# Sparse attention and a feed-forward block on one core: the tiles of two heads alternate, and both heads' products with v run as plain float32 on the two column halves of TensorE

## The chip, the core and the metric

The kernel runs on one core of a Trainium2 chip. The core has a matrix engine (TensorE, PE in the profile, with its weight loads as PEld), three engines for everything else (VectorE or DVE, ScalarE or ACT, GpSimd or POOL), a queue engine for DMAs (SyncE or SP), an on-chip memory (SBUF) of 128 partitions and a smaller one (PSUM) of eight banks, into which alone TensorE writes. The metric is the device time of one execution in microseconds. Engines run their own instruction lists in order and wait for each other by semaphores.

## What is computed

```python
def _attn_ref(q, k, v, tau):              # 8 batches, 8 heads, 576 positions, head size 64
    scores = np.matmul(q, k.transpose(0, 1, 3, 2)) / np.sqrt(64)
    thresh = np.max(scores, axis=-1, keepdims=True) - tau
    scores = np.where(scores >= thresh, scores, -1000000000.0)
    scores = scores - np.max(scores, axis=-1, keepdims=True)
    attn = np.exp(scores)
    attn = attn / (np.sum(attn, axis=-1, keepdims=True) + 1e-09)
    return np.matmul(attn, v)

def _moe_ref(x, w_in, w_out):             # 4608 tokens, 512 -> 2048 -> 512
    h = x @ w_in
    sp = np.where(h > 20.0, h, np.log1p(np.exp(np.minimum(h, 20.0))))
    return (h * np.tanh(sp)) @ w_out
```

The output of attention, heads side by side, is the input x of the second function. All is float32.

## The kernel before

**Stages.** Attention goes over 32 pairs of heads (four pairs a batch); the first large product (h, x times w_in) of one batch runs between the attention tiles of the next batch. When attention is over, the last batch's h follows, then the second large product (o). Only attention and the h among it are touched here.

**A pair and its tiles.** A pair has 2 x 576 = 1152 query rows, cut into nine tiles of 128 rows. `QCOL` says which columns of which head's q a tile takes: tiles 0 to 3 are head 0, tile 4 is the last 64 rows of head 0 and the first 64 of head 1, tiles 5 to 8 are head 1. Tiles are numbered through all pairs by g (0 to 287), and t = g % 9.

**A tile's way.** `begin` issues the scores s on PE (two PSUM tiles, so that s of g + 2 waits for the mask of g). DVE takes the row maximum (`st<-s`), ACT the exponential e, DVE masks and sums (p), POOL normalises. Two steps later PE transposes the tile in four pieces of 128 positions (`tp`, one PSUM tile) and the last 64 positions (t5, named t in the profile). A step later ACT copies the result to SBUF. The normalised tile of an even g stands in the left half of a buffer, that of an odd g in the right half; the scores of even g are computed with the last 64 positions in front (`first` is D), so that two tails lie side by side and one transposition serves two tiles.

**Two kinds of arithmetic.** Pairs 0 to 3 (`FULL`) multiply in plain float32. All others split each operand into a high part (float32r, one fast pass) and a remainder: ACT makes `hi`, DVE makes `lo` (lines 456 to 469), both for the four main pieces and for the tails (`tk`), and POOL and ACT split v into `vs` (128 columns: high and remainder).

**The products with v.** They come in four groups a pair, each of one head: 256, 320, 320 and 256 query rows (`WIDTH`), after tiles 1, 4, 6 and 8 (`LAST`). In pairs from 4 on a group is nine products (`values`): hi and lo for each of four chunks, tk for the last, all with 128 stationary columns. ACT copies the upper and the lower half out of PSUM (`x`, `yo`), POOL adds them. In pairs 0 to 3 a group is five plain products with 64 stationary columns (`values_full`), spread over steps by `PIECES`.

**The order.** One step of the loop (lines 668 to 768) is one g. On PE it issues s of g + 1, the group of products that has come due, so many h products as `MIX` says for this step (twelve h products fill one bank, which ACT then copies to `hst`), and the transpositions of g - 2 (during the first 38 steps these stand ahead of the products). The groups y and the h take turns at two PSUM banks (`psh`, tag `ph`). On ACT a step is: the copies of the transposed tile g - 3, the exponential of g, copies out of y, splits of loaded data, copies of h. `LOADS` gives the step in which each part of the next pair but one is loaded.

Of the kernel before, what the change touches and what calls it, by code (L numbers as in the profile page):

```python
# [17 lines left out]
LOADS = ((1, 0, 1, 3, 2, 3, 7, 3, 5, 8), (0, 3, 3, 2, 5, 4, 5, 8, 5, 7), (0, 0, 2, 4, 5, 4, 7, 6, 7, 8))  # L18
# [4 lines left out]
FIRST = (0, 4, 5, 1, 2, 6, 7, 3, 8, 9)  # L23
# [42 lines left out]
MIX_FIRST = (11, 12, 6, 9, 8, 13, 6, 14, 22, 6, 16, 4, 12, 4, 15, 9, 16, 13, 7, 12, 5, 10, 8, 13, 12, 14, 16, 6, 16, 4, 12, 4, 15, 5, 16, 13)  # L66
# [90 lines left out]
def attention_moe(tc, q, k, v, tau, w_in, w_out, out):  # L157
# [3 lines left out]
    with ExitStack() as outer:  # L161
# [105 lines left out]
        with ExitStack() as first:  # L267
# [6 lines left out]
            with ExitStack() as att:  # L274
# [36 lines left out]
                def prep(pi):  # L311
# [9 lines left out]
                    if full:  # L321
                        made["vf"] = ops.tile([P, 2, 5, D], F32, name="vf", tag="vs")
# [35 lines left out]
                    def v_part(a):  # L358
                        if full:
# [12 lines left out]
                        return split  # L372
# [6 lines left out]
                def scores(t, first, qs, k1, k2, plain, **_):  # L379
                    s = pss.tile([P, 2, 512], F32, name="s")  # L380
                    terms = []
                    if plain:
                        for n, (a, col) in enumerate(QCOL[t]):
                            for c in range(2):
                                rows = slice(c * D, (c + 1) * D)
                                nc.tensor.matmul(
                                    s[:, c, :HB], qs[a][rows, col:col + P], k1[a][rows, first:first + HB],
                                    start=n == 0, stop=n == len(QCOL[t]) - 1,
                                )
                        return s  # L390
                    for a, col in QCOL[t]:
# [37 lines left out]

                def transposes(g):  # L430

                    both = tiles[g]["both"]
                    odd = g % 2
                    at = odd * (S + D)
# [4 lines left out]
                    if g < FULL * 9:  # L439
                        t5 = pst.tile([P, P], F32, name="t5")  # L440
                        nc.tensor.transpose(t5[:D], both[:, 4 * P + odd * D:4 * P + (odd + 1) * D], ident)
                    elif odd:
                        t5 = pst.tile([P, P], F32, name="t5")
                        nc.tensor.transpose(t5, both[:, 4 * P:5 * P], ident)
                    return tp, t5

                def evacuate(t, tp, t5, pt):
                    for r, off, src, n in PLACE[t]:
                        if r not in pt:
                            pt[r] = [ptp.tile([P, w, 320], F32, name="pf", tag=tag) for w, tag in ((4, "hi"), (1, "tk"))]  # L450
                        main, tail = pt[r]
                        dst = slice(off, off + n)
                        nc.scalar.copy(main[:, :, dst], tp[:, :, src:src + n])
                        nc.scalar.copy(tail[:D, 0, dst], t5[:D, src:src + n])
# [33 lines left out]
                def values_full(r, pt, vf, x):  # L488
                    main, tail = pt.pop(r)
                    n = WIDTH[r]  # L490
                    a = r // 2
                    y = psh.tile([P, 512], F32, name="y", tag="ph")

                    def chunk(c):
                        if c < 4:
                            nc.tensor.matmul(y[:D, :n], vf[:, a, c], main[:, c, :n], start=c == 0, stop=False)
                        else:
                            nc.tensor.matmul(y[:D, :n], vf[:D, a, 4], tail[:D, 0, :n], start=False, stop=True)
# [125 lines left out]
                def start_pair(g, pi):  # L624
                    parts, todo = prep(pi)
                    pairs[pi] = dict(ops=parts, pt={})
                    for work, step in zip(todo, LOADS[1 if 2 <= pi < FULL + 2 else pi % 2 * 2]):
                        loads.setdefault(g + step, []).append(work)

                def begin(g):  # L630
                    pi, t = divmod(g, 9)
                    made = pairs[pi]["ops"]
                    tiles[g] = dict(s=scores(t, D if g % 2 == 0 else 0, **made))

                def product(g):
                    pi, t = divmod(g, 9)
                    pr = pairs[pi]
                    if t == 1:
                        pr["x"] = sm.tile([P, S], F32, name="x", bufs=2)
                    if t in LAST:  # L640
                        if pi < FULL:
                            some, gather = values_full(LAST[t], pr["pt"], pr["ops"]["vf"], pr["x"])
                            pieces.extend((work, None) for work in some[:-1])
                            pieces.append((some[-1], (gather, pi if t == 8 else None)))
                        else:
                            adds.append(values(LAST[t], pr["pt"], pr["ops"]["vs"], pr["x"]))

# [20 lines left out]
                for g in range(NT + 5):  # L668
# [4 lines left out]
                    ahead = 2 <= g < FULL * 9 + 2  # L673
                    lag = 4 if g < FULL * 9 + 4 else 5
                    if lag <= g < NT + lag and g != FULL * 9 + 4:
                        product(g - lag)
                    if 3 <= g < NT + 3:
                        old = ((g - 3) % 9, *tiles[g - 3]["tp"], pairs[(g - 3) // 9]["pt"])
                        full = g - 3 < FULL * 9
# [9 lines left out]
                    for _ in range(5 if g >= FULL * 9 + 3 else PIECES[g % 9]):  # L689
# [35 lines left out]
                    if g >= 12 + 9 * FULL and g % 9 == XSPLIT[0]:  # L725
# [17 lines left out]
                    if g < NT:  # L743
# [4 lines left out]
                        if g % 2 == 0:  # L748
                            both = sm.tile([P, 2 * S], F32, name="p", bufs=2)
                        tiles[g]["both"] = both  # L750
                        half = both[:, :S] if g % 2 == 0 else both[:, S:]
# [202 lines left out]
```

## Time and profile before

| | us |
|---|---|
| median of three runs (1333.97 to 1335.15) | 1335.02 |
| profiled execution | 1334.37 |
| its span | 1332.5 |
| tiles 0 to 41, first to last row maximum | 123.0 |
| tiles 42 to 287 | 762.2 |
| a steady batch of 36 tiles | 110.8 |

The profiled execution's span runs from its first to its last instruction; the 1.9 us between it and the execution's time lie around it. A row of the timeline gives start, duration and a group of equal instructions (out<-in, partitions times elements, count). On PE the ends are modelled and overlap the next start, so distances between starts tell what a matmul takes.

### The profile page before, as it was taken

The page shows a single profiled execution, that of the slowest core. Times are in us where ns is not written, and L with a number is a line of the kernel's source. Part 1 is how long each engine was busy: PE and PEld are TensorE (multiplying, and loading weights), DVE is VectorE, ACT ScalarE, POOL GpSimd, SP SyncE. Part 2 cuts the span into 40 slices and gives each one's busy share as a digit, 9 for nine tenths or more (in the row PEclk, how much of TensorE's full clock was granted, in tenths as well). Part 3 has the DMA queues.
Part 4 walks back from the last instruction along what each step waited for, and adds up shares of the span by engine and source line. Part 5 has one row for each costly group of instructions (what it writes and reads, how often), then busy time and mean ns, then how long its engine had stood idle before and what let it go on. Part 6 is the DMA issues. An engine that isn't in the chain of part 4 may idle for free.

```text
span 1332.5 us, 29620 instructions
## 1 busy us (share of the span) xinstructions
PE 1306.9 (98%) x9799; PEld 1232.8 (93%) x9799; DVE 1117.0 (84%) x2964; ACT 983.3 (74%) x2036; POOL 870.3 (65%) x1229
## 2 busy tenths in 40 slices
PE   8997999999999999999999999999999999999998
PEld 6445899999999999999999999999889999999998
DVE  6999999999999999999999999986986666667664
ACT  4888888888888888888888888875655555555552
POOL 3789998778788787887878878753403433543431
PEclk9999999999999999999999999999999999999999
DMA  5323463333333333333333333314744443444440
GB/s 179 103 81 119 113 189 105 107 97 106 103 102 109 96 106 104 101 110 95 106 104 101 113 92 106 99 37 137 244 130 159 134 136 120 134 135 135 143 127 33
DMA packets 151913, 154.90 MB, mean 116 GB/s; under 512 B 35536, under 2 KB 128720, under 8 KB 151760
## 3 DMA queue, kind: packets, MB, share of 16 engines
q1 hardware_dynamic: 151760, 153.00, 38.6%
q8 instruction: 78, 1.28, 0.4%
q14 instruction: 75, 0.61, 0.1%
HBM read 105.78 MB, written 47.19 MB: 115 GB/s over the span
## 4 chain that ended last, share of the span: by engine, by line
PE 90%; DVE 4%; ACT 3%; issue 1%; DMA 1%; POOL 1%; DVEq 0%; POOLq 0%; ACTq 0%
PE h L91 27%; PE o L91 27%; PE s L91 13%; PE y L91 12%; PE tp L91 9%; DVE st L91 1%; PE t L91 1%; ACT e L91 1%; DVE dec L91 1%; DVE p L91 1%; PE warm L91 0%; DVE w2l L91 0%; ACT w L91 0%; POOL s L91 0%; DMA hd<-hst 0%
## 5 line engine op out<-in xcount | busy, mean ns | idle before, releaser
L91 PE MATMUL h<-xh,w1h 128*128 128x288 f32 x1024 | 302.4, 295 | 1.0 <-ACT hst L91 0.9
L91 PE MATMUL h<-xl,w1h 128*128 128x288 f32 x1024 | 302.4, 295 | 0.0
L91 PE MATMUL h<-xh,w1l 128*128 128x288 f32 x1024 | 302.2, 295 | 0.0
L91 POOL TENSOR_SCALAR p<-p,st 128x576 f32<-128x576 f32 x288 | 242.4, 842 | 56.4 <-DVE st L91 30.7
L91 POOL TENSOR_TENSOR z<-z 128x256 f32<-128x256 f32 x128 | 126.1, 989 | 221.3 <-DVE z L91 212.5
L91 DVE SCALAR_TENSOR_TENSOR p<-s,st,e 128x576 f32<-128x576 f32 x288 | 235.1, 816 | 20.7 <-ACT e L91 10.7
L91 PE MATMUL s<-k,q 128*128 128x288 f32 (+1 forms) x1280 | 240.8, 332 | 9.0 <-DVE p L91 8.0
L91 ACT ACTIVATE e<-s,st 128x576 f32<-128x576 f32 x288 | 214.5, 745 | 32.2 <-DVE st L91 25.4
L91 DVE TENSOR_TENSOR gl<-z,gh 128x1792 fp32r<-128x1792 f32 (+1 forms) x72 | 141.3, 1963 | 107.7 <-ACT gh L91 107.7
L91 ACT CAST gh<-z 128x1792 fp32r<-128x1792 f32 (+1 forms) x72 | 116.5, 1620 | 150.2 <-issue 78.5
L91 DVE TENSOR_REDUCE st<-s 128x1 f32<-128x576 f32 x288 | 216.7, 752 | 2.1 <-PE s L91 2.1
L91 DVE TENSOR_TENSOR lo<-tp,hi 128x512 fp32r<-128x512 f32 (+1 forms) x280 | 174.8, 633 | 48.8 <-ACT hi L91 41.7
L91 PEld LDWEIGHTS s<-k,q 128*128 128x128 f32 (+1 forms) x1280 | 169.7, 189 | 35.3 <-DVE p L91 21.0
L91 PEld LDWEIGHTS h<-xh,w1h 128*128 128x128 f32 x1024 | 192.5, 188 | 1.6 <-ACT hst L91 1.6
L91 PEld LDWEIGHTS h<-xh,w1l 128*128 128x128 f32 x1024 | 192.5, 188 | 0.0
L91 PEld LDWEIGHTS h<-xl,w1h 128*128 128x128 f32 x1024 | 192.4, 188 | 0.0
L91 PE MATMUL tp<-ident,p 128*128 128x128 f32 x1152 | 175.2, 275 | 5.2 <-DVE lo L91 2.2
L91 ACT CAST hi<-tp 128x512 fp32r<-128x512 f32 (+1 forms) x280 | 149.8, 546 | 36.5 <-PE tp L91 33.7
L91 PEld LDWEIGHTS tp<-ident,p 128*128 128x128 f32 x1152 | 138.7, 140 | 19.9 <-issue 8.3
L91 POOL TENSOR_TENSOR x<-x,yo 64x256 f32<-64x256 f32 (+1 forms) x112 | 89.8, 802 | 87.8 <-ACT yo L91 85.5
L91 PE MATMUL o<-gh,sl 128*128 128x256 f32 x512 | 144.5, 282 | 0.0
L91 PE MATMUL o<-gl,sh 128*128 128x256 f32 x512 | 143.8, 281 | 0.0
(76 smaller groups left out, 3234.5 us busy)
## 6 DMA issues: line engine op xcount, KB each, us to landing
z<-hd SPq DMA_DIRECT2D x144, 256.0 KB, 3.1
r<-q SPq DMA_DIRECT2D x112, 160.0 KB, 2.3
r<-k SPq DMA_DIRECT2D x112, 160.0 KB, 2.2
out_t<-c SPq DMA_DIRECT2D x36, 256.0 KB, 2.4
r<-v SPq DMA_DIRECT2D x56, 160.0 KB, 2.3
dec<-w_in SPq DMA_DIRECT2D x32, 256.0 KB, 3.3
hd<-hst SPq DMA_DIRECT2D x16, 512.0 KB, 3.3
w<-w_out SPq DMA_DIRECT2D x16, 512.0 KB, 4.5
```

What stands on the lines that cost most here:

```text
L91: made = method(*args, **kwargs)
```

## The change

- All 32 pairs (`VP`) now keep v in float32 and multiply the normalised, transposed tile with it in plain float32. The splits of the transposed tile (lo and tk on DVE) and of v go. The scores stay as they were: plain in pairs 0 to 3, split in the others.
- Tiles of the two heads alternate (`TURN`): even t are head 0, odd t head 1, each with its own 128 rows; the mixed tile is now t = 8. ACT copies an even tile to `hi` and an odd one to `lo` (here just two buffers, one for each head); tails come in pairs, two extra transpositions serve tile 8.
- There are two groups a pair instead of four (`CLOSE`): 256 columns after t = 3, 320 after t = 8. A group has five chunks, and each chunk two products with 64 stationary columns, head 0 into partitions 0 to 63 and head 1 into 64 to 127 of the same bank. One copy takes all 128 partitions out; `yo` and the sums on POOL go.
- That copy is made one step after the group's last product (the list `ready`).
- The number of h a step is `EVEN`: 14, 14, 14, 0, 13, 14, 14, 0, 13 for g % 9 = 0 to 8, as many in all as `MIX`, with none in the two steps that hold a group.
- `LOADS` and `FIRST` bring the second head's q and k earlier; pairs 0 to 3 do two chunks a step (`PIECES`); p has three buffers.

In the steady part, a group on PE. Names: s scores, y a group's bank, vs or vf the values, hi, lo, tk the transposed tile, h the first large product. Before:

```order
L91 MATMUL y_11300<-hi_11084,vs_10608 128x320 [waits Activation_49]
L91 MATMUL y_11300<-lo_11085,vs_10608 128x320
L91 MATMUL y_11300<-hi_11084,vs_10608 128x320
L91 MATMUL y_11300<-lo_11085,vs_10608 128x320
L91 MATMUL y_11300<-hi_11084,vs_10608 128x320
L91 MATMUL y_11300<-lo_11085,vs_10608 128x320
L91 MATMUL y_11300<-hi_11084,vs_10608 128x320
L91 MATMUL y_11300<-lo_11085,vs_10608 128x320
L91 MATMUL y_11300<-tk_11086,vs_10608 128x320
L91 MATMUL h_11286<-xl_8133,w1h_104 128x288
```

Now, the group of 320 columns (the step has no h, so transpositions follow):

```order
L95 MATMUL y_10934<-hi_10700,vf_9885 64x320 [waits Activation_49]
L95 MATMUL y_10934<-lo_10701,vf_9885 64x320
L95 MATMUL y_10934<-hi_10700,vf_9885 64x320
L95 MATMUL y_10934<-lo_10701,vf_9885 64x320
L95 MATMUL y_10934<-hi_10700,vf_9885 64x320
L95 MATMUL y_10934<-lo_10701,vf_9885 64x320
L95 MATMUL y_10934<-hi_10700,vf_9885 64x320
L95 MATMUL y_10934<-lo_10701,vf_9885 64x320
L95 MATMUL y_10934<-tk_10702,vf_9885 64x320 x2
L95 MATMUL tp_10966<-ident_84,p_10808 128x128 [waits Activation_49,Pool_49]
```

Nine products of one head have become ten of 64 columns, one of each head in turn.

The same place on ACT, where y leaves its bank (x). Before, the copies stand in the group's own step, ahead of the next tile's copy (hi):

```order
L91 ACTIVATE e_11315<-s_11252,st_11314 128x576 [waits DVE_49,Activation_49]
L91 COPY x_11141<-y_11300 64x320 [waits PE_49]
L91 COPY yo_11310<-y_11300 64x320 [waits Pool_49]
L91 CAST q0_11214<-r_11220 128x320 [waits DMAHW3_49]
L91 CAST q0_11214<-r_11222 128x320 [waits DMAHW4_49]
L91 COPY hst_11231<-h_11286 128x288 [waits PE_49]
L91 CAST hi_11362<-tp_11352 128x4x128 [waits PE_49]
```

Now:

```order
L95 COPY lo_10936<-tp_10966 128x4x128 [waits PE_49]
L95 COPY tk_10937<-t5_10971 128x128 [waits PE_49]
L95 ACTIVATE e_10981<-s_10929,st_10980 128x576 [waits DVE_49,Activation_49]
L95 COPY x_10698<-y_10934 128x320
L95 CAST xh_10990<-x_10698 128x288 [waits Activation_49]
L95 COPY hst_10912<-h_10914 128x288 [waits PE_49]
```

The copy out of y has moved behind the copies of the tile that PE transposes right after the group, and behind the next exponential.

And PE's rows from those transpositions to the next user of y's bank, which is h_11003 (its wait is for the copy x_10698):

```order
L95 MATMUL tp_10966<-ident_84,p_10808 128x128 [waits Activation_49,Pool_49]
L95 MATMUL tp_10966<-ident_84,p_10808 128x128 x3
L95 MATMUL t5_10971<-ident_84,p_10808 128x128
L95 MATMUL s_10973<-k11_10306,q1_10305 128x288 [waits DVE_49]
L95 MATMUL s_10973<-k21_10307,q1_10305 128x288
L95 MATMUL s_10973<-k11_10306,q1_10305 128x288
L95 MATMUL s_10973<-k21_10307,q1_10305 128x288
L95 MATMUL h_10914<-xh_10144,w1h_104 128x288
L95 MATMUL h_10914<-xl_10145,w1h_104 128x288
L95 MATMUL h_10914<-xh_10144,w1l_105 128x288
L95 MATMUL h_11003<-xh_8875,w1h_104 128x288 [waits PE_49,Activation_49]
```

Three h end the bank that was begun ahead of the group, and the fourth begins in y's bank. Before, the group above was followed by eleven h, the transpositions and the scores before h took that bank. After the group of 256 columns it is now ten h.

The diff, cut to its core:

```diff
-PIECES = (3, 3, 3, 3, 4, 2, 3, 4, 3)
+PIECES = 2
+VP = 32
+SOON = 9 * FULL + 2
+TURN = [[(t % 2, t // 2 * P + t % 2 * P)] for t in range(8)] + [QCOL[4]]
+CLOSE = {3: 0, 8: 1}
+EVEN = (14, 14, 14, 0, 13, 14, 14, 0, 13)
...
+                    whole = pi < VP
+                    made["cols"] = TURN if whole else QCOL
...
+                def odd(g):
+                    return (g % 9 if g < 9 * VP else g) % 2
...
+                    last = g < 9 * VP and g % 9 == 8
+                    if odd(g) or last:
                         t5 = pst.tile([P, P], F32, name="t5")
+                        if last:
+                            nc.tensor.transpose(t5, both[:, S - P:S], ident)
+                            nc.tensor.transpose(t5[:D], both[:, S - D:S], ident)
+                        else:
+                            nc.tensor.transpose(t5, both[:, 4 * P:5 * P], ident)
...
                 def evacuate(t, tp, t5, pt):
...
+                    if t < 8:
+                        a, at = t % 2, t // 2 % 2 * P
+                        nc.scalar.copy(pt[r][a][:, :, at:at + P], tp)
+                        if a:
+                            nc.scalar.copy(tail[:, at:at + P], t5)
+                        return
+                    for a in range(2):
+                        rows = slice(a * D, (a + 1) * D)
+                        nc.scalar.copy(pt[r][a][:, :, 2 * P:], tp[:, :, rows])
+                        nc.scalar.copy(tail[rows, 2 * P:], t5[rows, rows])
...
                     def chunk(c):
+                        for a in range(2):
+                            rows = slice(a * D, (a + 1) * D)
+                            if c < 4:
+                                w, m = vf[:, a, c], main[a][:, c, :n]
+                            else:
+                                w, m = vf[rows, a, 4], tail[rows, 0, :n]
+                            nc.tensor.matmul(y[rows, :n], w, m, start=c == 0, stop=c == 4)
 
                     def gather():
-                        nc.scalar.copy(x[a * D:a * D + D, XOFF[r]:XOFF[r] + n], y[:D, :n])
+                        nc.scalar.copy(x[:, r * QT:r * QT + n], y[:, :n])
...
-                        advance(stream, DRAIN if g >= NT else MIX_FIRST[(step + 6) % 36] if b == 1 else MIX[g % 18] if b < B - 1 else MIX_LAST[step])
+                        advance(stream, DRAIN if g >= NT else EVEN[g % 9] if b == 1 or VP == NPAIRS else MIX[g % 18] if b < B - 1 else MIX_LAST[step])
```

More of the change, by code (lines that the diff above doesn't have):

```diff
@@ L358, in v_part @@
                     def v_part(a):
-                        if full:
+                        if whole:
                             nc.sync.dma_start(made["vf"][:, a], v[pi, :, a])
@@ L377, in prep, with scores @@
                     return made, loads
-                def scores(t, first, qs, k1, k2, plain, **_):
+                def scores(t, first, qs, k1, k2, plain, cols, **_):
                     s = pss.tile([P, 2, 512], F32, name="s")
@@ L387, in scores @@
                                     s[:, c, :HB], qs[a][rows, col:col + P], k1[a][rows, first:first + HB],
-                                    start=n == 0, stop=n == len(QCOL[t]) - 1,
+                                    start=n == 0, stop=n == len(cols[t]) - 1,
                                 )
                         return s
-                    for a, col in QCOL[t]:
+                    for a, col in cols[t]:
                         cs = slice(col, col + P)
@@ L438, in transposes @@
                     t5 = None
-                    if g < FULL * 9:
+                    last = g < 9 * VP and g % 9 == 8
+                    if odd(g) or last:
                         t5 = pst.tile([P, P], F32, name="t5")
[L441 to L444, printed above, removed]
+                        if last:
[3 more added lines that the diff above has]
+                            nc.tensor.transpose(t5, both[:, 4 * P:5 * P], ident)
                     return tp, t5
                 def evacuate(t, tp, t5, pt):
[L448 to L454, printed above, removed]
+                    r = t // 4 if t < 8 else 1
+                    if r not in pt:
+                        pt[r] = [
+                            ptp.tile([P, w, 320], F32, name=n, tag=n) for n, w in (("hi", 4), ("lo", 4), ("tk", 1))
+                        ]
+                    tail = pt[r][2][:, 0]
+                    if t < 8:
[8 more added lines that the diff above has]
+                        nc.scalar.copy(tail[rows, 2 * P:], t5[rows, rows])
                 def evacuate_hi(t, tp, t5, pt):
@@ L488, in values_full @@
                 def values_full(r, pt, vf, x):
-                    main, tail = pt.pop(r)
-                    n = WIDTH[r]
-                    a = r // 2
+                    main, tail = pt[r][:2], pt.pop(r)[2]
+                    n = (2 + r) * P - r * D
                     y = psh.tile([P, 512], F32, name="y", tag="ph")
                     def chunk(c):
[L495 to L498, printed above, removed]
+                        for a in range(2):
[5 more added lines that the diff above has]
+                            nc.tensor.matmul(y[rows, :n], w, m, start=c == 0, stop=c == 4)
                     def gather():
-                        nc.scalar.copy(x[a * D:a * D + D, XOFF[r]:XOFF[r] + n], y[:D, :n])
+                        nc.scalar.copy(x[:, r * QT:r * QT + n], y[:, :n])
                     return [lambda c=c: chunk(c) for c in range(5)], gather
@@ L626, in start_pair @@
                     pairs[pi] = dict(ops=parts, pt={})
-                    for work, step in zip(todo, LOADS[1 if 2 <= pi < FULL + 2 else pi % 2 * 2]):
+                    for work, step in zip(todo, LOADS[1 if 2 <= pi < FULL else 3 if FULL <= pi < VP else pi % 2 * 2]):
                         loads.setdefault(g + step, []).append(work)
@@ L632, in begin @@
                     made = pairs[pi]["ops"]
-                    tiles[g] = dict(s=scores(t, D if g % 2 == 0 else 0, **made))
+                    tiles[g] = dict(s=scores(t, 0 if odd(g) else D, **made))
                 def product(g):
@@ L672, in attention_moe @@
                         begin(g + 1)
-                    ahead = 2 <= g < FULL * 9 + 2
-                    lag = 4 if g < FULL * 9 + 4 else 5
-                    if lag <= g < NT + lag and g != FULL * 9 + 4:
+                    ahead = 2 <= g < SOON
+                    lag = 4 if g < VP * 9 + 4 or VP == NPAIRS else 5
+                    if lag <= g < NT + lag and (g != VP * 9 + 4 or VP == NPAIRS):
                         product(g - lag)
@@ L688, in attention_moe @@
                     ready.clear()
-                    for _ in range(5 if g >= FULL * 9 + 3 else PIECES[g % 9]):
+                    for _ in range(5 if g >= SOON else PIECES):
                         if pieces:
@@ L747, in attention_moe @@
                                     work[2]()
-                        if g % 2 == 0:
-                            both = sm.tile([P, 2 * S], F32, name="p", bufs=2)
+                        if not odd(g):
+                            both = sm.tile([P, 2 * S], F32, name="p", bufs=3)
                         tiles[g]["both"] = both
-                        half = both[:, :S] if g % 2 == 0 else both[:, S:]
+                        half = both[:, S:] if odd(g) else both[:, :S]
                         tiles[g]["p"] = masked(g, tiles[g]["s"], tiles[g]["st"], tiles[g]["e"], half)
```

28 lines of the change are left out of this document (13 added, 15 removed).

## The prediction

> **What bounds the kernel now.** I read the page first, then the busy time by stretches, then the waits of one steady stretch, then the timelines of TensorE and ScalarE.
>
> ```profile
> PE 1306.9 (98%) x9799; PEld 1232.8 (93%) x9799; DVE 1117.0 (84%) x2964; ACT 983.3 (74%) x2036; POOL 870.3 (65%) x1229
> ...
> PE 90%; DVE 4%; ACT 3%; issue 1%; DMA 1%; POOL 1%; DVEq 0%; POOLq 0%; ACTq 0%
> 6.94:109.57 102.63, 96.00 (x525) 51.26 (x522) 91.92 (x319) 81.17 (x203) 74.65 (x113) 1.00 0.41 125
> 109.57:129.97 20.40, 16.60 (x84) 10.00 (x81) 19.60 (x61) 16.12 (x40) 18.71 (x29) 0.96 0.30 84
> 341.34:452.10 110.76, 110.75 (x852) 109.27 (x851) 101.97 (x333) 94.73 (x229) 89.91 (x137) 1.00 0.37 104
> 784.45:892.15 107.70, 107.69 (x834) 106.77 (x833) 99.56 (x327) 90.01 (x216) 80.58 (x125) 1.00 0.30 87
> PEld s L91 <- DVE p L91: 1.2, 6, 0.2
> ```
>
> The second row is the chain that ended last: nine tenths of it is PE. The next four rows are stretches (length, then busy us of PE, PEld, DVE, ACT, POOL, then clock), cut where VectorE begins the row maxima of tiles 0, 36, 42, 252 and 287 (the third is one batch, tiles 108 to 143). In the steady stretch of 36 tiles PE is busy 110.75 of 110.76 us, while DVE has 9 us to spare. The last row is the only wait of TensorE in that stretch: 1.2 us. So from tile 42 on the pace is what TensorE has to do: 110.76 / 4 = 27.69 us a pair of heads. Relief of DVE, ACT and POOL buys there at most the 0.30 us a pair of that wait. In the first stretch (2.85 us a tile) two things share the limit, and its floor can be read between two row maxima of neighbouring tiles:
>
> ```profile
> 68.30 0.75 DVE L91 TENSOR_REDUCE st<-s 128x1 f32<-128x576 f32 x1
> ...
> 70.85 0.75 DVE L91 TENSOR_REDUCE st<-s 128x1 f32<-128x576 f32 x1
> ```
>
> Maximum, exponential and mask of a tile follow each other at 2.55 us, whatever PE does.
>
> **The products with v, pair by pair.** First the price of a plain float32 record and of a change of tile shape, from pairs 0 to 3 (start, duration, group; a plain matmul leaves two records):
>
> ```profile
> 62.01 1.83 PE L91 MATMUL y<-pf,vf 128*64 128x320 f32 x6
> 63.77 0.76 PE L91 MATMUL s<-k,q 64*128 64x288 f32 x4
> 64.46 0.66 PE L91 MATMUL tp<-ident,p 128*128 128x128 f32 x4
> 64.95 0.27 PE L91 MATMUL t<-ident,p 128*64 128x128 f32 x1
> ...
> 66.51 1.24 PE L91 MATMUL s<-k,q 64*128 64x288 f32 x8
> 67.69 0.66 PE L91 MATMUL tp<-ident,p 128*128 128x128 f32 x4
> 68.18 0.27 PE L91 MATMUL t<-ident,p 128*64 128x128 f32 x1
> 68.38 1.51 PE L91 MATMUL y<-pf,vf 128*64 128x256 f32 x6
> 69.82 0.76 PE L91 MATMUL s<-k,q 64*128 64x288 f32 x4
> ...
> 71.20 1.22 PE L91 MATMUL y<-pf,vf 128*64 128x256 f32 x4
> 72.35 0.76 PE L91 MATMUL s<-k,q 64*128 64x288 f32 x4
> ...
> 73.73 1.08 PE L91 MATMUL y<-pf,vf 128*64 128x256 f32 x4
> 74.74 0.76 PE L91 MATMUL s<-k,q 64*128 64x288 f32 x4
> ```
>
> Only starts are used, since ends are modelled. Six records of 256 columns take 68.38 to 69.82 = 1.44, four take 73.73 to 74.74 = 1.01: 0.215 a record and 0.15 fixed. Six of 320 take 62.01 to 63.77 = 1.76, so (1.76 - 0.15) / 6 = 0.268 each. The four from 71.20 hold the short fifth chunk in another shape (64 rows) and take 1.15, so a change inside a group costs 0.14. The step into y is paid by the row ahead: t to y is 68.38 - 68.18 = 0.20, where a transposition next to another takes (64.95 - 64.46) / 4 less 0.055 for the first, 0.11: so 0.09. After y or s the first tp costs that 0.055 more.
>
> Do two halves run together? The scores of these pairs do it on row halves: four records of 288 take 64.46 - 63.77 = 0.69, eight take 67.69 - 66.51 = 1.18, so four more cost 0.49. One record of 288 should take 0.215 x 288 / 256 = 0.242, so four cost two: full overlap. The fixed part is 0.20, 0.05 more than for one half. For column halves no row exists. The bounds are 1 and 2 times one half's time; I take 1, by the row-half rows, the nearest.
>
> So a group after the change: 10 record times (5 chunks, both heads side by side) of 0.215 or 0.268, 2.15 and 2.68, plus 0.09 in, 0.14 inside, 0.15 fixed, 0.055 behind, and 2 x 0.05 for the second half's load at two entries: 0.54. A pair has one group of each width: 4.83 + 1.08 = 5.91 us. The bounds for the changes are 0.44 a group (no second load) and about 0.64 (each entry another 0.05). Before:
>
> ```profile
> 305.15 0.28 PE L91 MATMUL y<-hi,vs 128*128 128x256 f32 x1
> ...
> 306.22 0.29 PE L91 MATMUL h<-xh,w1h 128*128 128x288 f32 x1
> ...
> 307.81 0.60 PE L91 MATMUL tp<-ident,p 128*128 128x128 f32 x4
> ...
> 396.67 0.60 PE L91 MATMUL tp<-ident,p 128*128 128x128 f32 x4
> 397.10 0.27 PE L91 MATMUL t<-ident,p 128*128 128x128 f32 x1
> 397.13 0.77 PE L91 MATMUL s<-k,q 128*128 128x288 f32 x4
> 397.74 0.31 PE L91 MATMUL y<-hi,vs 128*128 128x320 f32 x1
> ...
> 399.06 0.29 PE L91 MATMUL h<-xl,w1h 128*128 128x288 f32 x1
> ```
>
> Nine split products take 306.22 - 305.15 = 1.07 at 256 columns and 399.06 - 397.74 = 1.32 at 320. A pair has two of each: 4.78. So **y costs 1.13 us more a pair**: four plain passes for two heads at once do not beat two split products for one head each. The tails go from 4.5 to 6 transpositions a pair, (397.10 - 396.67) / 4 = 0.11 each: **+0.16**. The wait for DVE goes (-0.30): lo and tk leave DVE, and the shortest step now carries 13 h.
>
> **A new wait.** The group y of 320 columns leaves its PSUM bank only in the next step, behind two copies and an exponential on ACT, and after three h the next h group wants that bank (the rows are in the section on the change). ACT's times:
>
> ```profile
> 397.30 0.59 ACT L91 CAST hi<-tp 128x512 fp32r<-128x512 f32 x1 [0.17 <-PE tp L91]
> 397.78 0.53 ACT L91 CAST tk<-t 64x128 fp32r<-64x128 f32 x2
> 398.34 0.74 ACT L91 ACTIVATE e<-s,st 128x576 f32<-128x576 f32 x1
> 399.25 0.42 ACT L91 COPY x<-y 64x320 f32<-64x320 f32 x1 [0.17 <-PE y L91]
> ...
> 392.41 0.74 ACT L91 ACTIVATE e<-s,st 128x576 f32<-128x576 f32 x1
> 393.05 0.42 ACT L91 CAST xh<-x 128x288 fp32r<-128x288 f32 x1
> ...
> L91 ACT COPY x<-y 64x256 f32<-64x256 f32 x64 | 23.5, 367 | 9.4 <-PE y L91 9.0
> ...
> 886.09 0.08 DVE L91 DVE_READ_ACCUMULATOR p<-s,st,e 128x1 f32 x1
> ...
> 886.22 0.56 PEld L91 LDWEIGHTS s<-k,q 128*128 128x128 f32 x4 [0.18 <-DVE p L91]
> ```
>
> Count from the start of t (397.10). ACT: the copy starts 0.20 later and lasts 0.48 to the next start; a tail 0.28 (half of 398.34 - 397.78), an exponential 0.64 (393.05 - 392.41), the gather 0.42: it ends at 2.02, and PE starts 0.05 after what it waits for (DVE's sum ends at 886.17, s loads at 886.22): 2.07. PE: s starts 0.03 later and takes 0.61; three h at (307.81 - 306.22) / 12 = 0.1325 take 0.40: it is ready at 1.04. **PE stands still 1.03 us a pair.** Behind the waiting h stand in PE's queue nine more h of that group, the next tile's transpositions and scores, and ACT's next copy waits for those. At the 256 group ten h come first: PE is ready at 0.03 + 0.61 + 1.33 = 1.97, ACT, whose gather is then 0.37 long, at 1.97 and 0.05: it waits 0.05. Bounds for the two: 0, should the gather come in time, and 1.3, should a cast stand ahead on ACT.
>
> **Sum.** A pair: 1.13 + 0.16 - 0.30 + 1.08 = +2.07, so 29.76. Tiles 42 to 287 are 246 / 9 = 27.33 pairs, 813.4, less 3.1 because the last batch ran that much below the steady one (110.76 - 107.70): 810.3 against 892.15 - 129.97 = 762.2, +48.1. Ahead of that, 42 tiles took 123.0; their floor is 42 x 2.55 = 107.1. PE's y there halves (the four pairs' groups are 64 columns wide and alone), but the decoding of w1 stays on DVE and overfills some tiles: I take half of the gain, -8, bounds -16 and 0. What else moves is hidden: ACT loses a copy of y per group, POOL its sums x and the split of v; neither is waited for by PE today, so they bring nothing more; loads of v move by one to three steps and are needed ten steps later; at the very start the second head's q and k are now loaded third to sixth, for tile 1, in time if they land ahead of the second row maximum. The end from tile 288 on is unchanged.
>
> The profiled execution took 1334.37 us (span 1332.5): 1334.4 + 48.1 - 8 = 1374.5. It lies 0.65 below the median of the runs, so I say **1375 us**.
>
> ```profile
> 120.00:135.00 15.00, 11.68 (x57) 9.22 (x56) 14.52 (x41) 11.99 (x30) 14.02 (x21) 0.78 0.40 113
> ```
>
> The clock fell to 0.78 in the one stretch where PE had work for 11.68 of 15 us. After the change PE has less to do in all of the start: s 0.69, tp 0.49, t 0.07 and y 0.66 make 1.91 of 2.55 us a tile. The Trainium skill (TensorE: Matmul & The Clock Gate, Part 1, What's actually happening) says that the clock halves after an idle window of about 3.4 us and recovers after a busy one; by that rule the start could lose its gain, and the sum would be 1383.
>
> **Rivals.**
> *The bank is free in time (0.20).* The mechanism is the gather on ACT. If its chain is shorter than PE's three h, the 1.08 go: +0.99 a pair, 27.33 x 28.68 - 3.1 - 762.2 = +18.5, less 8: 1345. With the low ends of the rest (changes at 0.44, start at its floor) it is +0.79 and -16: 1331, faster than before; with these ends it decides at 0.11 us of wait a pair. For it: no h waits for ACT in the steady stretch today. Against: today eleven h, tp and s lie between y and the next user of its bank.
> *The halves take turns (0.09).* Then y is 2 x 4.83 + 2 x 0.44 = 10.54 a pair, +6.70 in all: 27.33 x 34.39 - 3.1 - 762.2 = +174.6, no gain at the start: 1509. The change would then not do what it says. For it: no row shows column halves. Against: row halves overlap in full.
> *They overlap in part (0.07).* If both halves' streams hinder each other by a quarter, their time grows to 6.04 a pair: +3.28 in all, 27.33 x 30.97 - 3.1 - 762.2 = +81.1, less 8: 1408. The Trainium skill (TensorE: Matmul & The Clock Gate, Part 3, Measured speedup vs the span model) gives 2.38 times for three column tiles, not 3; taken as a rate it asks for 1.26 times the record time, about this rival. That it counts the time of a single pack, start and end included, speaks against reading it so, and the row halves' 0.49 shows no such loss.
>
> **How the numbers follow.** The forecast has 0.64. Its own ends are 1353 (changes 0.44, 0.8 of wait, start at the floor) and 1394 (changes 0.64, wait 1.3, no gain at the start). The range goes down to the first rival's low end, less what a measurement may differ, and leaves out the other two: 1328 to 1394. A measurement can tell 0.2%, 2.7 us, from no change. Faster by more: 0.11 and within it 0.06, both from the first rival; slower 0.83 from all the rest.
>
> **What would show it.** In the profile after: y records of the two heads starting in twos within hundredths, 0.215 and 0.268 apart (halves together); y groups of 2.7 and 3.2 us; PE h waiting for ACT x about once a pair for 1 us; 36 tiles in 119 us; row maxima of the start at 2.55 to 2.9 us; no lo and no tk on DVE. I am wrong if no h waits for x, or if a y group is near 2.2 or over 4 us.

## The result, and the profile after

The changed kernel takes 1378.51 us (median of four runs, 1377.15 to 1379.66), the kernel before 1335.09 in the runs beside it: a ratio of 1.0326, 95% interval 1.0314 to 1.0339. It is slower by 3.3%, 3.5 us above the forecast of 1375. The profiled execution took 1377.15.

First the page: busy time of the engines, and the costliest groups that answer to the forecast.

```profile
PE 1318.8 (96%) x9941; PEld 1164.4 (85%) x9941; DVE 878.1 (64%) x2404; ACT 848.0 (62%) x1676; POOL 736.9 (54%) x1061
...
L95 PE MATMUL h<-xh,w1h 128*128 128x288 f32 x1024 | 306.7, 299 | 23.3 <-ACT x L95 21.7
...
L95 PE MATMUL y<-hi,vf 128*64 128x320 f32 (+1 forms) x512 | 144.6, 424 | 1.0 <-ACT hst L95 1.0
```

The change does what it says: DVE loses 239 us of work, ACT 135, POOL 133, and PE, which set the pace, gains 12 busy us and a new idle time. The last field of the h row is that time: 21.7 us before h groups, for ACT's copy x. The y row is one of the two heads; the other's is like it (144.5), and their busy times overlap, so 289 us of y are not 289 us of PE.

Next the busy time by stretches: two of the start and one steady batch (tiles 108 to 143).

```profile
30.00:60.00 30.00, 25.94 (x154) 13.16 (x152) 28.00 (x95) 21.96 (x54) 23.67 (x37) 0.89 0.36 112
60.00:90.00 30.00, 24.11 (x140) 12.35 (x136) 28.60 (x101) 24.17 (x62) 23.99 (x36) 0.88 0.24 75
...
346.98:464.69 117.71, 114.61 (x874) 100.50 (x873) 67.47 (x253) 76.28 (x181) 71.03 (x112) 1.00 0.34 97
```

The steady batch went from 110.76 to 117.71 us: +1.74 a pair. PE is idle for 3.1 us of it, where before the view showed 0.01. In the start PE is busy for 25.94 and 24.11 of 30 us, the clock falls to 0.88, and DVE is nearly full (28.60 of 30).

Where the steady 1.74 come from stands in PE's timeline of one pair (start, duration, group; in brackets the engine's idle time just before it and what ended it):

```profile
400.51 0.43 PE L95 MATMUL y<-hi,vf 128*64 128x256 f32 x1
400.52 0.43 PE L95 MATMUL y<-lo,vf 128*64 128x256 f32 x1
400.78 0.38 PE L95 MATMUL y<-hi,vf 128*64 128x256 f32 x1
...
402.07 0.38 PE L95 MATMUL y<-hi,vf 128*64 128x256 f32 x1
...
402.39 0.65 PE L95 MATMUL y<-tk,vf 64*64 64x256 f32 x4
402.97 0.66 PE L95 MATMUL tp<-ident,p 128*128 128x128 f32 x4
...
415.01 0.77 PE L95 MATMUL s<-k,q 128*128 128x288 f32 x4
415.71 0.48 PE L95 MATMUL y<-hi,vf 128*64 128x320 f32 x1
...
418.70 0.66 PE L95 MATMUL tp<-ident,p 128*128 128x128 f32 x4
...
419.22 0.77 PE L95 MATMUL s<-k,q 128*128 128x288 f32 x4
...
420.08 0.30 PE L95 MATMUL h<-xh,w1l 128*128 128x288 f32 x1
421.15 0.40 PE L95 MATMUL h<-xh,w1h 128*128 128x288 f32 x1 [0.78 <-ACT x L95]
421.40 0.30 PE L95 MATMUL h<-xl,w1h 128*128 128x288 f32 x1
```

The two heads start 0.01 apart, and from the second pair of records on the next pair comes 0.215 later (400.78 to 402.07 is six of them: 1.29). A group of 256 columns takes 402.97 - 400.51 = 2.46, one of 320 takes 418.70 - 415.71 = 2.99. Three h follow the tile's transpositions and scores, and the fourth starts 1.07 after the third instead of 0.13.

ACT at the same place:

```profile
419.39 0.59 ACT L95 COPY lo<-tp 128x512 f32<-128x512 f32 x1 [2.13 <-PE tp L95]
419.87 0.27 ACT L95 COPY tk<-t 128x128 f32<-128x128 f32 x1
420.03 0.76 ACT L95 ACTIVATE e<-s,st 128x576 f32<-128x576 f32 x1
420.67 0.44 ACT L95 COPY x<-y 128x320 f32<-128x320 f32 x1
```

ACT stood idle for 2.13 us while PE did y; then came a copy of tp, a tail, an exponential, and only then x, whose end (421.11) lets h start at 421.15.

### The profile page after: what moved, and what is told of

Read it like the earlier page. It is cut to its first block, busy times and chain, and to the rows that moved or that the text cites. A ratio compares the mean times of both kernels' runs of the same rounds, so it can differ in the third digit from the quotient of the medians.

```text
span 1375.4 us, 28492 instructions
## 1 busy us (share of the span) xinstructions
PE 1318.8 (96%) x9941; PEld 1164.4 (85%) x9941; DVE 878.1 (64%) x2404; ACT 848.0 (62%) x1676; POOL 736.9 (54%) x1061
## 3 DMA queue, kind: packets, MB, share of 16 engines
q8 instruction: 79, 1.29, 0.4%
## 5 line engine op out<-in xcount | busy, mean ns | idle before, releaser
L95 PE MATMUL h<-xh,w1h 128*128 128x288 f32 x1024 | 306.7, 299 | 23.3 <-ACT x L95 21.7
L95 PE MATMUL tp<-ident,p 128*128 128x128 f32 x1152 | 179.3, 278 | 3.0 <-POOL p L95 1.2
L95 ACT COPY lo<-tp 128x512 f32<-128x512 f32 (+1 forms) x160 | 87.1, 545 | 151.5 <-PE tp L95 150.4
L95 PEld LDWEIGHTS tp<-ident,p 128*128 128x128 f32 x1152 | 135.4, 141 | 43.4 <-issue 31.0
L95 ACT COPY hi<-tp 128x512 f32<-128x512 f32 (+1 forms) x160 | 87.1, 545 | 100.5 <-PE tp L95 100.4
L95 PE MATMUL y<-hi,vf 128*64 128x320 f32 (+1 forms) x512 | 144.6, 424 | 1.0 <-ACT hst L95 1.0
L95 PE MATMUL y<-lo,vf 128*64 128x320 f32 (+1 forms) x512 | 144.5, 424 | 0.0
L95 PE MATMUL o<-gh,sl 128*128 128x256 f32 x512 | 144.5, 282 | 0.0
```

The source lines that it names most:

```text
L95: made = method(*args, **kwargs)
```

## The experiments

All twelve are edits of the changed kernel, and are called by their numbers below. A ratio is to the kernel before, run beside each; its 95% interval follows. The stretches cut the trace at the row maxima of the same tiles as before.

**One: the copy out of y in the group's own step.**

```diff
                     done = list(ready)
                     ready.clear()
...
+                    if g >= SOON:
+                        done += ready
+                        ready.clear()
                     if g < NT:
                         tiles[g]["st"], tiles[g]["e"] = row_max(tiles[g]["s"])
```

> The copy out of y stands in the group's own step again, right behind that step's exponential on ACT, as before the change; all else as in the changed kernel. If the h group behind the 320-column group waits for that copy (the profile after shows 0.94 us more than a plain distance once a pair), the wait goes: 27.33 x 0.94 = 26 us less than the changed kernel, about 1353 us, and h no longer waits for ACT x. Rival: the wait only moves, because ACT now stands still for the end of y and comes late to the next tile's copy and exponential, so that s waits for DVE instead: about 1365 us or more, with a wait of PE s for DVE p in its place.

Measured: 1363.03 us, ratio 1.0197 (1.0179 to 1.0216); a batch takes 115.83. No h waits for x any more, but another wait is there. Its row in the waits of a steady stretch (us in total, times, longest), then a step after a group of 320 columns on ACT, DVE and PE:

```profile
PEld s L95 <- DVE p L95: 2.4, 4, 0.6
```
```profile
414.76 0.43 ACT L95 COPY x<-y 128x320 f32<-128x320 f32 x1 [2.26 <-PE y L95]
415.09 0.46 ACT L95 CAST q<-r 128x320 fp32r<-128x320 f32 x1
...
415.81 0.43 ACT L95 CAST xh<-x 128x288 fp32r<-128x288 f32 x1
416.14 0.58 ACT L95 COPY lo<-tp 128x512 f32<-128x512 f32 x1
...
416.77 0.76 ACT L95 ACTIVATE e<-s,st 128x576 f32<-128x576 f32 x1
...
417.57 0.82 DVE L95 SCALAR_TENSOR_TENSOR p<-s,st,e 128x576 f32<-128x576 f32 x1 [3.16 <-ACT e L95]
...
418.45 0.81 PE L95 MATMUL s<-k,q 128*128 128x288 f32 x4 [0.35 <-DVE p L95]
```

Half of the gain went into a wait of 0.6 us a pair: two casts (q, k), which ACT did during y before, and the cast xh now stand between x and the copy of tp. The exponential is late, DVE's p with it, and s waits for p. So both expectations came in part: the wait of h goes, and the rival's wait of s takes half of the gain.

**Two: h dealt so that each waiting point has work ahead of it.** The copy stays a step later; the steps ahead of the next user of y's bank get other numbers of h.

```diff
-EVEN = (14, 14, 14, 0, 13, 14, 14, 0, 13)
+EVEN = (12, 12, 12, 0, 17, 17, 14, 0, 12)
```

> The copy out of y stays a step late, but the h are dealt out as 12, 12, 12, 0, 17, 17, 14, 0, 12, so that ten h instead of three stand between the 320-column group and the h group that takes its bank (as many h in all). If the wait is for the bank, it goes as in the run with the copy in its own step: about 26 us less than the changed kernel, 1353 us. Rival: it is the chain of copy, exponential and mask on ACT and DVE that is late there, whatever bank the h take: no change, 1378 us.

Measured: 1358.75 us, ratio 1.0171 (1.0147 to 1.0195); a batch takes 114.80, 0.73 a pair less. In the view no h waits for x any more, with the copy where it was: it is the bank that h waited for, and PE's order decides it. What is left of the expected 26 us (20 came) is a wait of s in the steps that now hold 12 h, and the h behind the first in each of y's banks, which still starts late (0.24 after 320 columns, 0.19 after 256, instead of 0.13). The wait in a steady stretch, then the h after 320 columns:

```profile
PEld s L95 <- DVE p L95: 0.6, 4, 0.2
```
```profile
386.85 0.40 PE L95 MATMUL h<-xh,w1h 128*128 128x288 f32 x1
387.09 0.30 PE L95 MATMUL h<-xl,w1h 128*128 128x288 f32 x1
```

**Three: the fifth chunk in the shape of the others.** The fifth chunk is multiplied over all 128 rows, with zeros in v's layout where the other head's tail lies; nothing else is computed.

```diff
-                                w, m = vf[rows, a, 4], tail[rows, 0, :n]
+                                w, m = vf[:, a, 4], tail[:, 0, :n]
...
-    vp = np.empty((B, NP, P, 2, 5, D), f)
+    vp = np.zeros((B, NP, P, 2, 5, D), f)
...
-        vp[:, :, a * D:(a + 1) * D, :, 4] = vt[:, :, :, 512:].transpose(0, 1, 3, 2, 4)
+        vp[:, :, a * D:(a + 1) * D, a, 4] = vt[:, :, a, 512:]
```

> The fifth chunk of a group runs over all 128 rows, with zeros in the rows of v that belong to the other head, so that the shape of the tile (128 rows, 64 columns) does not change inside a group; passes and columns stay the same. If a change of shape costs 0.10 us on the way and 0.05 on the first record, two groups a pair save 2 x 0.14: 27.33 x 0.28 = 7.7 us less than the changed kernel, about 1371 us, and the distance from the fourth chunk to the fifth falls from 0.36 to 0.26 at 320 columns. Rival: the fifth chunk waits for its weights or its tail and not for the shape: no change, 1378 us.

Measured: 1370.32 us, ratio 1.0254 (1.0234 to 1.0273); a batch takes 116.53, 0.29 a pair less. Its group of 256 columns:

```profile
400.08 0.43 PE L95 MATMUL y<-hi,vf 128*64 128x256 f32 x1
...
401.65 0.38 PE L95 MATMUL y<-lo,vf 128*64 128x256 f32 x1
401.86 0.60 PE L95 MATMUL y<-tk,vf 128*64 128x256 f32 x4
402.39 0.66 PE L95 MATMUL tp<-ident,p 128*128 128x128 f32 x4
```

2.31 instead of 2.46: tk starts 0.21 after the last pair instead of 0.32. A change of shape inside a group costs 0.15, as the prediction read it from the start of before (0.14). The expectation holds, at 320 columns too (tk 0.26 after the last pair).

**Four: the halves one behind the other.** All five chunks of head 0, then those of head 1.

```diff
-                    def chunk(c):
-                        for a in range(2):
+                    def chunk(k):
+                        for a, c in (divmod(2 * k, 5), divmod(2 * k + 1, 5)):
```

> The same ten products of a group, but all five of head 0 ahead of all five of head 1, so that no two neighbours stand on different column halves. If the halves overlap only as neighbours, the records are paid one by one: about 4.8 us more a pair and one more change of shape a group (0.14), 27.33 x 5.1 = 139 us more than the changed kernel, about 1517 us. Rival: TensorE pairs them anyway over several products, or the overlap never carried the time: 1378 to 1450 us.

Measured: 1532.33 us in its one run, 15 above the expectation; a batch takes 139.26. The same group of 256 columns:

```profile
487.90 1.94 PE L95 MATMUL y<-hi,vf 128*64 128x256 f32 x8
...
490.35 1.94 PE L95 MATMUL y<-lo,vf 128*64 128x256 f32 x8
...
492.79 0.66 PE L95 MATMUL tp<-ident,p 128*128 128x128 f32 x4
```

2.45 for the one head and 2.44 for the other, where both together took 2.46. The overlap is whole where the two halves alternate in PE's list, and there is none where each half's products stand together.

**Five: more work for PE in the start.** Transpositions into a bank that nobody reads, in steps 10 to 41, so that the clock stays up.

```diff
-WARM = (24, (26, 12, 6, 4, 3, 2, 2, 2, 2, 2))
+WARM = (24, (26, 12, 6, 4, 3, 2, 2, 2, 2, 2) + tuple((4, 8, 8, 0, 0, 4, 8, 0, 0)[g % 9] if g < 39 else 8 for g in range(10, 42)))
```

> The changed kernel with transpositions of the identity that nobody reads on TensorE in those steps of tiles 10 to 41 that hold no product with v (4 or 8 a step), so that the granted clock stays full there; before, it fell to a half once in the start (6.8 us), after four times (27 us). If that is what ate the start's gain, tiles 0 to 41 fall from 123.6 us to about 115 and the kernel to about 1370 us. Rival: the start is bound by VectorE's chain and by the decoding of w1 on it (DVE is busy 28.0 and 28.6 of 30 us there), so the clock does not matter: 123 us again and 1378 us.

Measured: 1375.65 us, ratio 1.0298 (1.0280 to 1.0315). Tiles 0 to 41:

```profile
7.59:128.65 121.06, 104.74 (x727) 66.18 (x723) 110.30 (x372) 88.87 (x215) 92.73 (x140) 1.00 0.40 123
```

The clock is 1.00, and the start is 2.5 us shorter, no more (123.6 to 121.1). DVE is busy for 110.30 of 121.06, nearly what it was before (91.92 + 19.60 in the same tiles). So the rival holds but for those 2.5 us: with PE's work and its clock out, DVE is the engine left that is nearly full. That it sets the pace is argued from this; no run takes work off it there. The waits of 6 to 130 us say the same, in the kernel before and in the changed one (us in total, times, longest): what PE no longer has to do, it waits for DVE's p.

```profile
PE s L91 <- DVE p L91: 4.7, 8, 1.1
```
```profile
PE s L95 <- DVE p L95: 18.3, 21, 1.5
```

**Six and eight: the plain products in the first four pairs alone,** as in the kernel before, but in the new order of tiles; in eight also with the h of the second batch dealt by the old table (`MIX_FIRST`).

```diff
-VP = 32
+VP = 4
...
```

> Only pairs 0 to 3 take alternating tiles and column halves (VP = 4); from pair 4 on the split products, the tile order and the MIX of before, save that the second batch keeps the even deal of h. If the loss is made from tile 42 on by the plain products and the late copy, a steady batch is 110.8 us again and the kernel within 5 us of the kernel before, 1335 to 1342 us. Rival: the new start costs of itself, or the steady pace hangs on other edits (three buffers for p, loads): over 1345 us.

> As the run with column halves in pairs 0 to 3 alone, with the second batch's deal of h of before as well. If the start's halved products with v are worth what the chain lets through, tiles 0 to 41 take 120 to 124 us and the kernel 1332 to 1337 us, no different from before; were they hidden work only, exactly that. Rival: the start gains its 8 us here, 1327 us.

Measured: 1358.39 us (ratio 1.0167, 1.0145 to 1.0190) and 1341.58 (1.0044, 1.0027 to 1.0062). Two stretches of six (tiles 42 to 71, a steady batch), then tiles 42 to 71 of eight:

```profile
133.00:250.37 117.37, 101.18 (x696) 95.36 (x696) 96.12 (x305) 85.91 (x214) 90.83 (x135) 0.94 0.40 119
364.55:475.28 110.73, 110.73 (x852) 109.28 (x851) 101.93 (x333) 94.62 (x228) 89.90 (x137) 1.00 0.37 104
```
```profile
131.49:236.93 105.44, 98.03 (x706) 94.60 (x706) 97.69 (x305) 85.28 (x214) 90.69 (x135) 0.95 0.44 132
```

The steady pace of before is back to 0.03 us: what the steady part lost lies in what `VP` takes back (the products with v, their groups, the order of tiles and the late copy), and not in what stays, such as the third buffer of p. Both expectations of the whole missed. In six the rival's time came (over 1345), but by neither of its causes alone: the start is 2.2 us longer, the steady pace is that of before, and most is lost in tiles 42 to 71. With the split products DVE has 96 to 98 us of work in those 30 tiles (before 95.5 of 100.6), and the even deal of h leaves PE waiting there (busy 101.18 of 117.37). The old deal mends most of it, not all.

**Nine: eight, with the unread transpositions of five.**

> The kernel of e8 (plain products in four pairs alone, the old deal of h in the second batch) with the unread transpositions of e5 in steps 10 to 41. In e8 the start took 124.8 us (before 123.0) and tiles 42 to 72 took 105.4 (before 100.6), with spells of half clock at 39.2, 76.7, 90.4, 114.3, 127.9 and 141.6 us. Theory A: those spells are what is left of e8's distance to the kernel before. Then the start comes to about 122.3 (e5 gained 2.5), tiles 42 to 72 to 101 to 102, and the time to 1335 to 1337. Theory B: the order of the tiles and the deal of h cost there by themselves, and the clock only follows from PE standing idle. Then the start gains 2 us or less, tiles 42 to 72 stay within 1 us of 105.4, and the time is 1339 to 1341.

Measured: 1339.19 us, ratio 1.0022 (1.0013 to 1.0031); tiles 0 to 41 take 125.2, tiles 42 to 71 103.1, at clocks of 0.99 and 0.98. Theory B for the start; in tiles 42 to 71 neither theory fits, as 2.4 of the 4.9 us lost go while the clock there rises from 0.95 to 0.98. What the new order costs in the four pairs beyond that (the start is 2 us longer than before, and the unread transpositions take PE time themselves) stays open.

**Seven: the repairs of two, three and five together.**

> The changed kernel with the deal of h of the second run, the full-row fifth chunk of the third and the filled start: all that can be taken off the new way without giving it up. If the extra passes and the two remaining changes of shape a group are what is left, a steady batch is 117.7 - 2.9 - 1.2 = 113.6 us and the kernel 1378 - 20 - 9 = 1349 us, less what the start gives: still slower than before by 0.6 to 1.1%. Rival: freed of both waits PE runs at the pace of before: 1335 us or less.

Measured: 1348.94 us, ratio 1.0101 (1.0083 to 1.0118); a batch takes 113.65. The three gains add up, and the rival is out.

**Ten and eleven: the copy last in its step.** Behind the casts, the copy out of y would wait in time that ACT has free. Ten is this alone:

```diff
                     for work in chores.pop(g, []):
                         work()
+                    while g >= SOON and ready:
+                        gather, closed = ready.pop(0)
+                        gather()
+                        if closed is not None:
+                            close_pair(g, closed)
```

> The changed kernel with the copy out of y in the group's own step, as in e1, but as the last copy of that step on ACT, behind the casts of q and k, which then fall into the time in which ACT waits for y anyway; the cast xh stays behind the next exponential. Theory: in e1 half of the gain went because three casts (3 x 0.36 us) stood between the copy and the next copy of tp, so that an exponential, and with it DVE's p, came late. Then neither h nor s waits here: the 0.94 us a pair go in full, a batch takes 113.9 to 114.1 us, tiles 42 to 287 about 777, the time is 1353 to 1355. Rival: the copy in the group's own step holds ACT up by itself (it stands waiting for y while it could work); then the wait of s stays as in e1, a batch takes 115.5 to 116 and the time is 1361 to 1364.

> e10 with the full-row fifth chunk of e3 (zeros in v's layout) and the unread transpositions of e5. If the three add up (0.94 and 0.29 us a pair, 2.5 us in the start): a batch of 112.7 to 112.9 us and 1343 to 1345. What would be left is the y of 5.44 a pair (5.73 less 0.29) against 4.78, the tails' 0.16, less the 0.30 of the old wait: +0.52 a pair, so slower than before all the same, by 0.5 to 0.7%. If e10's rival holds, 1351 to 1354.

Measured: 1346.61 us (ratio 1.0083, 1.0064 to 1.0101) and 1335.74 (1.0000, 0.9991 to 1.0010). Steady batch of ten, its copy x on ACT, and the steady batch of eleven:

```profile
338.71:452.04 113.33, 113.33 (x875) 100.29 (x873) 67.49 (x253) 76.67 (x181) 71.03 (x112) 1.00 0.35 101
```
```profile
408.30 0.43 ACT L95 COPY x<-y 128x320 f32<-128x320 f32 x1 [1.56 <-PE y L95]
```
```profile
335.19:447.35 112.16, 112.16 (x875) 101.05 (x874) 67.50 (x253) 76.76 (x181) 71.16 (x112) 1.00 0.36 102
```

PE is busy throughout, and neither h nor s waits: the theory holds, and the rival (ACT held up by its wait) does not. Both gained more than expected. A pair lost 1.10 us to the wait, not the 0.94 of the gap: (117.71 - 113.33) / 4. The rest is the slow start of what follows: the h behind the waiting one starts 0.25 later instead of 0.13 (421.15 to 421.40), and in the bank of a 256 group the second h was late by 0.06 too. Of the 246 tiles from 42 on, ten saves 30.3 us and eleven 38.3. What eleven still pays in a steady batch, (112.16 - 110.76) / 4 = 0.35 a pair, is the sum of what is left: y 0.95 less 0.29, the tails' 0.16, less 0.46 for the old wait (both sizes are worked out in the next section).

**Twelve: eleven with the plain products in pairs 0 to 7.** In pairs 8 to 31 the zeros of three now lie where the split product expects a second copy of v's last 64 rows, so part of the product with these rows is left out there; the instructions and the bytes are those of the full computation.

```diff
-VP = 32
+VP = 8
```

> The kernel of e11 with the plain products in pairs 0 to 7 alone; from pair 8 on the arithmetic, the four groups a pair and the deal of h of the kernel before. Theory: the plain products pay where PE does not set the pace (e11 took 121.5 us for the start against 123.0 and 93.9 for tiles 42 to 72 against 100.6), and cost 0.35 us a pair where it does. Then the time is e11's first 72 tiles with the steady part of before: 1336 less 24 pairs of 0.35, 1327 to 1330, faster than before by 0.4 to 0.7%; the steady batch takes 110.8 again. Rival: changing from one kind to the other in the middle of the run costs as much as in e6 and e8, where tiles 42 to 72 took 105 us and more; then tiles 72 to 102 take 5 us or more longer than in the kernel before, and the time is 1333 or more.

Measured: 1327.55 us, ratio 0.9937 (0.9924 to 0.9951). Tiles 0 to 41, 42 to 71, 72 to 107, 108 to 143:

```profile
7.68:128.65 120.97, 104.64 (x727) 66.29 (x723) 110.43 (x374) 89.05 (x215) 92.61 (x140) 1.00 0.40 123
128.65:223.00 94.35, 93.94 (x727) 83.98 (x728) 68.08 (x237) 70.99 (x173) 75.65 (x114) 1.00 0.48 143
223.00:334.86 111.86, 111.75 (x857) 108.32 (x855) 98.58 (x326) 92.39 (x224) 87.58 (x134) 1.00 0.35 101
334.86:445.62 110.76, 110.76 (x852) 109.29 (x851) 101.96 (x335) 94.65 (x229) 89.90 (x137) 1.00 0.36 103
```

Against the kernel before: 2.1 and 6.2 us saved in the first two stretches, 1.1 lost at the change of kinds, the pace of before from there on. The theory holds. With zeros in the layout of the first eight pairs only, it would compute the whole; that was not run.

## Why the prediction was right, and where its terms were off

| | forecast | measured |
|---|---|---|
| y, a pair | +1.13 | +0.95 |
| tails, a pair | +0.16 | +0.16 |
| old wait of s for p, a pair | -0.30 | -0.46 |
| new wait of h for x, a pair | +1.08 | +1.10 |
| sum, a pair | +2.07 | +1.75 (batch: +1.74) |
| tiles 42 to 287 | +48.1 | +39.3 |
| tiles 0 to 41 | -8 | +0.6 |
| up to the first row maximum, and from tile 287 on | 0 | -0.6 and +3.5 |
| profiled execution | 1374.5 | 1377.15 |

**The halves run together.** Right, and it was the step with the largest price: experiment four shows what the serial order costs, 154 us. The row halves of the scores in before had been the right stand-in. The signs named ahead came: y records in twos, and one h a pair waiting for x. The rival of a part overlap is out: 0.215 and 0.268 a record were forecast, 0.215 and (417.64 - 416.03) / 6 = 0.268 came, at both heads. The Trainium skill's 2.38 times for three column tiles (TensorE: Matmul & The Clock Gate, Part 3, Measured speedup vs the span model) is thus no rate for two halves of plain float32.

**A group's fixed part** was forecast at 0.54; it is 2.46 - 2.15 = 0.31 inside, 0.09 in (s to y 0.70, s to h 0.61) and 0.05 behind: 0.45. The term that was wrong is "2 x 0.05 for the second half's load": the distances leave no room for it. Its low end, 0.44 a group, was the value. So y is 5.73 a pair, and 4.78 before. What makes the loss is plain then: ten record times of both widths are 4.83, almost the old 4.78; the shape changes and entries around only two groups are nearly all of the +0.95.

**The new wait** was found before it existed, by counting two queues from the same start. Its gap was 0.94 instead of 1.03, as one tail copy of 128 rows takes 0.16 on ACT (419.87 to 420.03) where one cast of 64 rows took 0.28; with the slow start behind a wait it cost 1.10. Experiments two and ten show the cause from both sides: more work for PE ahead of the bank's next user, or an earlier copy, and it is gone. The rival in which the bank is free in time was therefore a matter of order, and experiment ten is that rival's kernel (+0.64 a pair, where the rival reckoned +0.99 with the terms as forecast).

**The old wait** was mis-sized in the same manner: the view of waits counted only the gap. By distances of starts, the step from tp to s took 2.05 us in the 18 steps of before's steady batch without a tail, where 0.028 each is usual, and the s behind took 0.29 us more in all than after: (2.05 - 18 x 0.028 + 0.29) / 4 = 0.46.

**Tiles 42 to 71** were not a term of their own. Before they took 100.6 us, 8 more than at the steady pace; the forecast let that excess go by putting all 246 tiles at one pace, and so it came (99.4 us, where 30 tiles at the steady pace are 98.1). No step of the prediction argues for it, so that is luck. It says that from tile 42 on TensorE sets the pace and that relief of DVE buys 0.30 us a pair at most; in these tiles before, PE was busy 96.88 and DVE 95.48 of 100.58 us, and relief of DVE bought more.

**The start** is the step that failed: "I take half of the gain, -8". PE's work fell and nothing was gained; DVE's work did not fall. The floor of 2.55 us a tile holds only while the decoding of w1 fits beside it. Two row maxima of after:

```profile
61.93 0.75 DVE L95 TENSOR_REDUCE st<-s 128x1 f32<-128x576 f32 x1
...
63.57 0.42 DVE L95 SCALAR_TENSOR_TENSOR dec<-dec 128x256 uint32<-128x256 uint32 x1
64.04 0.82 DVE L95 SCALAR_TENSOR_TENSOR p<-s,st,e 128x576 f32<-128x576 f32 x1
...
64.78 0.75 DVE L95 TENSOR_REDUCE st<-s 128x1 f32<-128x576 f32 x1
```

2.85 us, and the decoding fills all of the time between the maximum's small operations and p. The prediction saw DVE full in a part of the start (14.52 of 15) and still took half. The clock did fall, in four spells of 6.8 us at half speed, where before had one, from 128.3 us on, most of it behind tile 41. The 3.41 us ahead of the first spell, and the spell:

```profile
35.01:38.42 3.41, 1.87 (x13) 0.93 (x11) 2.89 (x11) 3.36 (x11) 2.28 (x4) 1.00 0.00 0
38.42:45.25 6.83, 5.92 (x21) 2.70 (x21) 6.51 (x22) 4.63 (x11) 5.72 (x9) 0.50 0.24 82
```

Ahead of the other three PE is busy 1.80, 1.75 and 1.44 us in as long a time, and its longest idle time from 10 to 129 us is 1.5 us. The rule that the prediction cites from the Trainium skill (TensorE: Matmul & The Clock Gate, Part 1, What's actually happening) speaks of an idle window of about 3.4 us; the trace shows none ahead of these spells, only windows about half filled. The start lost its gain as in the sum by that rule (1383), but the clock is little of it: experiment five took the spells away and gained 2.5 us of the 8.6 that were missed.

**The end** was not unchanged (+3.5): from the row maximum of tile 287 on PE has 466 records of h to do instead of 456, as `EVEN` also deals the last batch; 10 x 0.1325 = 1.3 us. What makes the other 2.2 stays open.

That the sum came within 0.2% is luck: 8.8 too much from tile 42 on, 8.6 too little in the start. The sign and the mechanism of the steady part are not.

## What to carry to other kernels

Taking a fifth of its work off an engine that nobody waits for buys nothing: price a change at the engine that is full in that stage, and apply it only in the stages where another one is. Here the plain products, with the repairs of eleven, gained 6.2 us in tiles 42 to 71, where DVE was nearly as full as PE, and lost 0.35 us a pair in the batches after them. Where a copy moves to a later step, count both queues from one common start up to the next user of the buffer, and look for a slot in the copying engine's list in which it waits anyway; the place of that one copy decided 32 us here (1378.5 to 1346.6).

## What was not expected of the hardware

- A wait costs PE more than its gap: the next matmul too starts late (0.25 for 0.13), which made 1.06 of 0.94. It comes without a gap too: in experiment two, 0.24 for 0.13 behind an h that starts on time, 0.05 after x ends (386.80).
- Two column halves of plain float32 overlap in full, starts 0.01 us apart, when their matmuls alternate, and not at all when each half's matmuls stand together (2.45 + 2.44 against 2.46).
- Four spells of half clock, 6.8 us each, came in a start in which PE's records cover 24 to 26 of 30 us and PE, from 10 us on, never stood idle for more than 1.5 us; each came behind 3.41 us in which PE was busy for 1.44 to 1.87. Unread transpositions in these steps (PE busy 104.74 of 121.06 us, where it was 100.7 of 123.6) removed them.
